# Weights in contiguous tiles, the first pair of the scan ahead of them, and low weight parts by TensorE

## The chip, the cores and the metric

The kernel runs on one core of one Trainium2 chip. What counts is the device time of the whole launch in microseconds; the median of several runs stands for a kernel. Inside the core five engines run their own in-order streams: TensorE (PE, with its weight loads PEld), VectorE (DVE), ScalarE (ACT), GpSimd (POOL) and SyncE (SP), which here issues all DMAs. They meet only at semaphores.

## The reference

The work is a gated linear attention (a complex-valued scan over time) followed by two MLPs. The MLP weights come as float64, which the kernel handles as pairs of 32-bit words.

```python
scale = min(mag, 0.999) / (mag + 1e-06)          # mag = |a_re + i a_im|
for t in range(768):                             # B=4, H=8, D=48
    new_re = ar * S_re - ai * S_im
    new_im = ar * S_im + ai * S_re
    S_re, S_im = new_re + k_t v_t^T, new_im
    y[:, :, t] = q_t @ S_re
x = y.transpose(0, 2, 1, 3).reshape(3072, 384)
x = square(relu(x @ w_in)) @ w_out               # w_in 384x2048
xn = x / rms(x) * rms_g
out = (silu(xn @ w_gate) * (xn @ w_val)) @ w_out2  # w_gate 384x1536
```

## The kernel before, in words

Time is cut into chunks of 128 steps, which makes 24 units (4 batches of 6 chunks); two units make a pair. For each pair `load_a`, `load_qk` and `load_v` bring the inputs, and a chain on VectorE and ScalarE works on the decay factors: `norm` (L131 to L155), seven times `step` (L165 to L170), `tot` (a TensorE product, L178), `blocks` (L199 to L206), `back` (L217), `apply` (L242 to L244) and `inv` (L255 to L258). Then each unit runs `kq` (the products KP and QP, L264), four turnings on TensorE (`dtr`, L286, copied out by ScalarE at L288), `score` (L298, copied at L300 and masked by GpSimd at L301), `do_y` (L314, copied as xt at L321), `fix` (six small transfers that regroup rows, L605), `state` (L332 to L346), and `split_x`, which cuts xt into a high part (ScalarE, L541) and a low part (VectorE, L542), called xs.

Two units make a group of 256 tokens for the first MLP: for each of the 16 blocks f of 128 hidden columns nine products of `mlp_h` (L620) and six of `mlp_x` (L637), with ScalarE and VectorE forming the high and low parts gs in between. All matrix products use such pairs (high x high, high x low, low x high) in the fp32r type. The second MLP has groups of three units and starts when the scan is done.

A weight tile of 128x384 has to be converted before use: a transfer lands the 64-bit words in `ws`, and `convert_f32` cuts them to 32 bits with one ScalarE step (L359), one GpSimd step (L360) and two VectorE steps (L363, L364) in one of two buffers `cr`; then ScalarE casts the high part (L541) and VectorE subtracts it to get the low part (L542). The first MLP has 32 such tiles, 16 of `w_in` and 16 of `w_out`. A `w_in` tile takes four transfers, since its rows are regrouped (`PIECES`, L560); a `w_out` tile takes one (L568). The second MLP has 36 tiles.

The order on each engine is not written by hand. Every step is entered with a time and a priority (`at(t, fn, ..., p=)`), the list is sorted by t, and a scheduler places the instructions by the priorities and by its own idea of what is free. `PSH`, `USH` and `WSH` shift the priorities of pair steps, unit steps and first-MLP conversions; the smaller number goes first.

Of the kernel before, what the change touches and what calls it, by code (L numbers as in the profile page):

```python
# [8 lines left out]
F32 = mybir.dt.float32  # L9
# [21 lines left out]
PSH, USH, WSH = -12, -4, -30  # L31
LOADA, LOADQ = -5, 7.5
YMAX2 = 3e4
GROUPS = [[2 * i, 2 * i + 1] for i in range(12)]
# [10 lines left out]
class Attention:  # L45
# [8 lines left out]
    def __init__(self, ctx, tc, q, k, v, a_re, a_im, ident, sb, ps, dram):  # L54
# [6 lines left out]
        self.V = [c.tile([128, H, 64], F32, name=f"V{i}") for i in range(2)]  # L61
# [10 lines left out]
    def init(self, mn):  # L72
# [13 lines left out]
        for t in self.V:  # L86
            nc.vector.memset(t[:, :, D:64], 0.0)
# [217 lines left out]
    def yy(self, u, xt):  # L305
# [5 lines left out]
        for p in range(4):  # L311
            for z in range(2):
                h = 2 * p + z
                nc.tensor.matmul(P[64 * z:64 * z + 64, p], lhsT=V[:, h, :], rhs=ST[:, h, :], start=True, stop=(c == 0))  # L314
# [8 lines left out]
    def state(self, u):  # L323
# [6 lines left out]
        for h in range(H):  # L330
            for lo, hi in ((0, 64), (64, 112)):
                nc.tensor.matmul(P[lo:hi, h], lhsT=kt[:, h, lo:hi], rhs=V[:, h, 0:D], start=True, stop=True)  # L332
# [48 lines left out]
def general_path(tc, q, k, v, a_re, a_im, w_in, w_out, w_gate, w_val, w_out2, ident, gcol, out):  # L381
# [3 lines left out]
    with ExitStack() as ctx:  # L385
        dram = ctx.enter_context(tc.tile_pool(name="g_dram", bufs=1, space=DRAM))
        xd = dram.tile([NT, DM], F32, name="g_xd")
        with ExitStack() as c1:
# [9 lines left out]
            with tc.For_i(0, S_LEN // T, 1) as it:  # L398
# [7 lines left out]
                for z in range(DQ):  # L406
                    nc.sync.dma_start(
                        vt[32 * z:32 * z + 32], v[:, :, bass.ds(it * T, T), :].rearrange("b h t d -> (b h) t d")
                    )
                re, im = tl["re"], tl["im"]  # L410
                flat = [t.rearrange("p t d -> p (t d)") for t in (re, im)]
                m, n, w = [sb.tile([128, T * DI], F32, name=f"g_m{i}") for i in range(3)]
# [34 lines left out]
        with ExitStack() as c2:  # L447
# [3 lines left out]
            def cols(w, f):  # L451
                st = sb.tile([128, KT, 256], I32, tag="gst", name="g_st", bufs=2)
                nc.sync.dma_start(st, w[:, 256 * f:256 * (f + 1)].rearrange("(k p) f -> p k f", p=128))
                return convert_f32(nc, sb, st.rearrange("p k n -> p (k n)")).rearrange("p (k n) -> p k n", k=KT)

            def rows(w, f):
                st = sb.tile([128, 2 * DM], I32, tag="gst", name="g_st", bufs=2)
                nc.sync.dma_start(st, w[128 * f:128 * (f + 1)])
                return convert_f32(nc, sb, st)
# [20 lines left out]
            with tc.For_i(0, NT // 128, 1) as it:  # L480
                x = sb.tile([128, DM], F32, tag="gx", name="g_x")
                nc.sync.dma_start(x, xd[bass.ds(it * 128, 128), :])
                xt = turned(x, None)
                acc = ps.tile([128, DM], F32, tag="gacc", name="g_acc")
                for f in range(F1):
                    hp = mm3(cols(w_in, f), xt, "gh")
# [3 lines left out]
                    nc.tensor.matmul(acc, lhsT=g, rhs=rows(w_out, f), start=(f == 0), stop=(f == F1 - 1))  # L490
# [8 lines left out]
                for f in range(F2):  # L499
                    gp = mm3(cols(w_gate, f), xt, "gh")  # L500
                    vp = mm3(cols(w_val, f), xt, "gv")
# [3 lines left out]
                    nc.tensor.matmul(acc, lhsT=g, rhs=rows(w_out2, f), start=(f == 0), stop=(f == F2 - 1))  # L505
# [6 lines left out]
def kernel_body(ctx: ExitStack, tc, q, k, v, a_re, a_im, w_in, w_out, w_gate, w_val, w_out2, rms_g, out):  # L512
    nc = tc.nc
    events = []
    w_in, w_out, w_gate, w_val, w_out2 = [t.bitcast(I32) for t in (w_in, w_out, w_gate, w_val, w_out2)]
# [6 lines left out]
    ident = keep.tile([128, 128], F32, name="ident")  # L522
    gcol = keep.tile([128, KT], F32, name="gcol")
# [28 lines left out]
    def load_cols(src, f, pieces, pool=wp):  # L552
        w = stage(pool)
        st = w[2].rearrange("p (k n) -> p k n", k=KT)
        if pieces is None:
            nc.sync.dma_start(st, src[:, 256 * f:256 * (f + 1)].rearrange("(k p) f -> p k f", p=128))
        else:
            width = src.shape[1]
            for r0, cnt, base, step in pieces:
                nc.sync.dma_start(  # L560
                    st[r0:r0 + cnt],
                    bass.AP(src.tensor, base * width + 256 * f, [[width, cnt], [step * width, KT], [1, 256]]),
                )
        return w

    def load_rows(src, f, pool=wp):
        w = stage(pool)
        nc.sync.dma_start(w[2], src[f * 128:(f + 1) * 128])  # L568
        return w

    def convert(w):
# [3 lines left out]
        split(w[:, 0], w[:, 1], r, nc.vector)  # L575
# [3 lines left out]
    PIECES = ((0, 48, 0, 96), (48, 16, 288, 16), (64, 48, 48, 96), (112, 16, 336, 16))  # L579
# [4 lines left out]
    def load_w1(f):  # L584
        win[f] = load_cols(w_in, f, PIECES)
        wout[f] = load_rows(w_out, f)

    def convert1(f, rows):
        w = wout if rows else win
        w[f] = convert(w[f])  # L590
# [268 lines left out]
```

## Time and profile before

| what | value |
|---|---|
| median of the runs | 1184.83 us (lowest 1183.83) |
| profiled execution, its own time | 1183.78 us |
| profiled execution, span from first to last instruction | 1182.1 us |
| TensorE matmul busy | 1060.9 us (90%) |
| VectorE busy | 720.7 us (61%) |
| ScalarE busy | 653.6 us (55%) |
| mean granted TensorE clock | 0.989 of full |

The shares are means over stages that differ: the page's slices show TensorE idle at the left end and nearly full from the fifth slice on, and VectorE full in the first third. What happens at the left end is read from windows of time and from the timeline.

### The profile page before, as it was taken

Reading aid. Unit: us, or ns where it says so; the run is one execution under the profiler, and the core shown is the slowest. Engines: PE = TensorE matmul, PEld = TensorE weight load, DVE = VectorE, ACT = ScalarE, POOL = GpSimd, SP = SyncE. Lnnn points to the kernel's source line nnn. Section 1 sums busy time; section 2 is a strip of 40 time slices with the busy share of each in tenths; the row PEclk is TensorE's granted clock in tenths of the full one; section 3 lists DMA queues with packets and bytes.
Section 4 is the critical chain, followed back from the end, with each engine's and each line's share of the span. In section 5 each row is a group of like instructions: output and inputs, shape, how many; then the busy total and the mean of one; then the engine's idle time right before and its main releaser. Section 6 shows DMA issues by size and latency. Waiting matters only on the chain.

```text
span 1182.1 us, 20622 instructions
## 1 busy us (share of the span) xinstructions
PE 1060.9 (90%) x7778; PEld 1030.7 (87%) x7778; DVE 720.7 (61%) x1564; ACT 653.6 (55%) x1421; POOL 210.9 (18%) x246
## 2 busy tenths in 40 slices
PE   0015898999999999999999999999999999999997
PEld 0014788999999999999999999999999999999997
DVE  6999797988978779687842379932232323222222
ACT  4347576786786767877577676733232424222221
POOL 2335342323222333222200023200000000000000
PEclk9998799999999999999999999999999999999999
DMA  9933322423423234231100493000000000000000
GB/s 230 250 88 85 101 60 89 113 70 99 126 58 110 65 84 108 76 110 38 44 24 16 142 313 117 21 21 21 21 21 21 21 21 21 21 3 18 16 6 23
DMA packets 98748, 85.45 MB, mean 72 GB/s; under 512 B 53328, under 2 KB 92496, under 8 KB 98640
## 3 DMA queue, kind: packets, MB, share of 16 engines
q1 hardware_dynamic: 98640, 84.05, 25.3%
q8 instruction: 63, 1.03, 0.4%
q14 instruction: 45, 0.37, 0.1%
HBM read 64.23 MB, written 18.61 MB: 70 GB/s over the span
## 4 chain that ended last, share of the span: by engine, by line
PE 58%; DVE 17%; ACT 9%; issue 6%; DMA 6%; SPq 3%; POOL 2%; DVEq 0%; ACTq 0%; POOLq 0%
PE o L789 12%; PE v L771 11%; PE g L771 11%; PE h L620 8%; PE x L637 8%; DVE XY L165 2%; PE sps L298 2%; DMA ws<-in_moe_w_in 2%; SPq L605 2%; PE dps L286 1%; DMA ws<-in_moe_w_out 1%; DVE cr L363 1%; PE yps L314 1%; DVE cr L364 1%; ACT dq L288 1%
## 5 line engine op out<-in xcount | busy, mean ns | idle before, releaser
L620 PE MATMUL h<-xs,w 128*128 128x256 f32 x1728 | 331.3, 287 | 10.3 <-ACT xs L541 6.1
L637 PE MATMUL x<-w,gs 128*128 128x384 f32 x1152 | 315.1, 348 | 9.1 <-DVE gs L627 8.6
L620 PEld LDWEIGHTS h<-xs,w 128*128 128x128 f32 x1728 | 269.5, 192 | 14.0 <-ACT xs L541 6.5
L637 PEld LDWEIGHTS x<-w,gs 128*128 128x128 f32 x1152 | 202.1, 190 | 15.0 <-DVE gs L627 11.4
L777 DVE TENSOR_TENSOR uu<-t,v 128x384 f32<-128x384 f32 x96 | 52.9, 552 | 206.9 <-PE v L771 204.0
L771 PE MATMUL g<-ys,w 128*128 128x384 f32 x864 | 171.7, 339 | 0.0
L789 PE MATMUL o<-w,us 128*128 128x384 f32 x864 | 170.8, 340 | 0.1
L771 PE MATMUL v<-ys,w 128*128 128x384 f32 x864 | 170.5, 340 | 0.3 <-DVE uu L777 0.3
L771 PEld LDWEIGHTS v<-ys,w 128*128 128x128 f32 x864 | 153.1, 188 | 0.9 <-DVE uu L777 0.6
L771 PEld LDWEIGHTS g<-ys,w 128*128 128x128 f32 x864 | 153.5, 188 | 0.3 <-ACT t L775 0.3
L789 PEld LDWEIGHTS o<-w,us 128*128 128x128 f32 x864 | 151.8, 188 | 1.0 <-ACT us L541 0.4
L775 ACT ACTIVATE t<-g 128x384 f32<-128x384 f32 x96 | 47.0, 490 | 146.0 <-PE g L771 146.0
L627 DVE TENSOR_TENSOR gs<-h,gs 128x256 fp32r<-128x256 f32 x192 | 79.4, 417 | 77.4 <-ACT h L626 74.9
L541 ACT CAST us<-uu 128x384 fp32r<-128x384 f32 x96 | 49.2, 513 | 114.1 <-DVE uu L777 114.1
L623 ACT ACTIVATE r<-h 128x256 f32<-128x256 f32 x192 | 73.6, 386 | 61.1 <-PE h L620 60.3
L360 POOL TENSOR_SCALAR cr<-ws 128x384 f32<-128x384 f32 x68 | 56.4, 834 | 155.8 <-DVE w L542 94.4
L625 ACT ACTIVATE gs<-r 128x256 fp32r<-128x256 f32 x192 | 81.2, 423 | 3.8
L301 POOL TENSOR_SCALAR_AFFINE_SELECT st<-st 128x512 f32<-128x512 f32 x48 | 38.7, 811 | 232.4 <-ACT st L300 231.7
L542 DVE TENSOR_TENSOR us<-uu,us 128x384 fp32r<-128x384 f32 x96 | 54.3, 566 | 38.3 <-ACT us L541 38.3
L626 ACT ACTIVATE h<-r 128x256 f32<-128x256 f32 x192 | 73.1, 381 | 0.0
L178 PE MATMUL tot<-ident,A 128*48 128x128 f32 x96 | 9.1, 305 | 57.9 <-DVE A L169 57.9
L165 DVE TENSOR_TENSOR XY<-A 128x384 f32<-128x384 f32 x84 | 59.0, 702 | 1.0
(117 smaller groups left out, 1485.8 us busy)
## 6 DMA issues: line engine op xcount, KB each, us to landing
ws<-in_moe_w_out SPq DMA_DIRECT2D x28, 384.0 KB, 5.3
kb<-KP SPq DMA_DIRECT2D x20, 448.0 KB, 4.1
kt<-kb SPq DMA_DIRECT2D x20, 448.0 KB, 4.1
raw<-in_a_re SPq DMA_DIRECT2D x24, 192.0 KB, 3.1
raw<-in_a_im SPq DMA_DIRECT2D x24, 192.0 KB, 3.3
ws<-in_moe_w_in SPq DMA_DIRECT2D x32, 144.0 KB, 5.1
kin<-in_k SPq DMA_DIRECT2D x24, 192.0 KB, 4.3
qin<-in_q SPq DMA_DIRECT2D x24, 192.0 KB, 3.1
```

The source lines that it names most:

```text
L165: nc.vector.tensor_tensor(out=T, in0=v.unsqueeze(1).to_broadcast([128, 2, 2, 2 * D]), in1=w.unsqueeze(2).to_broadcast([128, 2, 2, 2 * D]), ...
L360: nc.gpsimd.tensor_scalar(out=s.bitcast(F32), in0=hi.bitcast(F32), scalar1=0.0, scalar2=1.0, op0=ALU.mult, op1=ALU.mult)
L542: el.tensor_tensor(out=lo, in0=src, in1=hi.bitcast(F32), op=ALU.subtract)
L620: nc.tensor.matmul(hp, lhsT=w[:, a, kk, :], rhs=xs[:, bb, kk, :], start=(i == 0), stop=(i == 8))
L623: nc.scalar.activation(out=r, in_=hp, func=AF.Relu)
L625: nc.scalar.activation(out=gs[:, 0], in_=r, func=AF.Square)
L626: nc.scalar.activation(out=hp, in_=r, func=AF.Square)
L627: nc.vector.tensor_tensor(out=gs[:, 1], in0=hp, in1=gs[:, 0].bitcast(F32), op=ALU.subtract)
L637: nc.tensor.matmul(x_ps[g][i], lhsT=gs[:, a, i * CH:(i + 1) * CH], rhs=w[:, bb, :], start=(f == 0 and n == 0), stop=(f == F1 - 1 and n == 2),)
L771: nc.tensor.matmul(P, lhsT=w[:, a, kk, :], rhs=ys[:, bb, kk, :], start=(i == 0), stop=(i == 8))
L777: nc.vector.tensor_tensor(out=uu, in0=t, in1=ps[1], op=ALU.mult)
L789: nc.tensor.matmul(o_ps[g][i], lhsT=us[:, a, i * CH:(i + 1) * CH], rhs=w[:, bb, :], start=(f == 0 and n == 0), stop=(f == F2 - 1 and n == 2),)
```

## The change

The host now lays all five weight matrices out as one array of 128x768-word tiles in the order of use, so that each tile, of either kind, is one transfer with 3 KB rows (`load`). V is laid out on the host too, one row of 384 numbers for a time step, and its tile has no gaps of zeros any more. The loads of pairs 0 and 1 and the steps of the first pair and its units get priorities of their own (`LOAD0`, `PAIR0`, `UNIT0`), ahead of the conversions; the conversions of the first MLP move from `WSH` -30 to -40. Last, the low part of a first-MLP weight tile is formed on TensorE: identity times the 32-bit weights in fp32, plus minus-identity times the high part in fp32r, summed in PSUM (in the buffers of `h`), and ScalarE copies the result out. The second MLP's tiles keep the VectorE subtraction. The path for unusual inputs, which does not run here, is adapted and left out below.

```diff
-PSH, USH, WSH = -12, -4, -30
+PSH, USH, WSH = -12, -4, -40
+PAIR0, UNIT0 = -60, -50
+LOAD0 = ((-64, -63, -62.5), (-36.35, -35.5, -35.2))
...
-        self.V = [c.tile([128, H, 64], F32, name=f"V{i}") for i in range(2)]
+        self.V = [c.tile([128, H * D + 16], F32, name=f"V{i}") for i in range(2)]
...
-            self.V[u % 2][:, :, 0:D],
-            self.v[b, :, c * CH:(c + 1) * CH, :].rearrange("h t e -> t h e"),
+            self.V[u % 2][:, 0:H * D], self.v[b, c * CH:(c + 1) * CH].rearrange("t h e -> t (h e)")
...
+    minus = keep.tile([128, 128], F32R, name="minus")
...
+    def load(n, pool=wp):
+        t = stage(pool)
+        nc.sync.dma_start(t[2], w[n])
+        return t
+
+    def convert(w, on_pe):
+
         pool, n, st = w
         r = convert_f32(nc, CV[0], st, "cr", CRB)
         w = pool.tile([128, 2, DM], F32R, tag=f"w{n}", name="w", bufs=1)
-        split(w[:, 0], w[:, 1], r, nc.vector)
+        if not on_pe:
+            split(w[:, 0], w[:, 1], r, nc.vector)
+            return w
+        nc.scalar.copy(out=w[:, 0], in_=r)
+        P = psh.tile([128, DM], F32, tag="h", name="lo")
+        nc.tensor.matmul(P, lhsT=ident, rhs=r, start=True, stop=False)
+        nc.tensor.matmul(P, lhsT=minus, rhs=w[:, 0], start=False, stop=True)
+        nc.scalar.copy(out=w[:, 1], in_=P)
         return w
...
     def load_w1(f):
-        win[f] = load_cols(w_in, f, PIECES)
-        wout[f] = load_rows(w_out, f)
+        win[f] = load(T_IN + f)
+        wout[f] = load(T_OUT + f)
...
-        at(F1 * (g - 3) + LOADA, att.load_a, g)
-        at(F1 * (g - 2) + LOADQ, att.load_qk, g)
+        t = F1 * (g - 3) + LOADA
+        at(t, att.load_a, g, p=LOAD0[g][0] if g < 2 else t)
+        t = F1 * (g - 2) + LOADQ
+        at(t, att.load_qk, g, p=LOAD0[g][1] if g < 2 else t)
         for fr, *op in PAIR:
             t = F1 * (g - 2 + fr)
-            at(t, getattr(att, op[0]), g, *op[1:], p=t + PSH)
+            at(t, getattr(att, op[0]), g, *op[1:], p=t + PSH if g else PAIR0 + 10 * fr)
...
+                p = t0 + F1 * fr + USH if g else UNIT0 + 3 * i + 4 * fr
```

In what order the engines get the work stands in the built programs. On SyncE's queue, at the very start, the kernel before has this (the first number in a shape is partitions):

```order
L108 DMA raw<-in_a_re 128x1x384 x2
L108 DMA raw<-in_a_im 128x1x384 x2
L560 DMA ws<-in_moe_w_in 48x3x256
L560 DMA ws<-in_moe_w_in 16x3x256
L560 DMA ws<-in_moe_w_in 48x3x256
L560 DMA ws<-in_moe_w_in 16x3x256
L568 DMA ws<-in_moe_w_out 128x768
```

and the changed kernel this:

```order
L112 DMA raw<-in_a_re 128x1x384 x2
L112 DMA raw<-in_a_im 128x1x384 x2
L120 DMA kin<-in_k 128x1x384 x2
L120 DMA qin<-in_q 128x1x384 x2
L126 DMA V_89<-in_v 128x384
L126 DMA V_90<-in_v 128x384
L563 DMA ws<-in_w 128x768 x16
L112 DMA raw<-in_a_re 128x1x384 x2
L112 DMA raw<-in_a_im 128x1x384 x2
L563 DMA ws<-in_w 128x768 x16
```

The inputs k, q and v of the first pair, which stood behind all weights, now stand ahead of the first one.

On VectorE, in the first pair's `norm` and first `step`, the kernel before has this:

```order
L149 TENSOR_TENSOR m<-m,A_86 128x768
L542 TENSOR_TENSOR w<-cr,w 128x384 x2
L150 SCALAR_TENSOR_TENSOR A_86<-m,A_86 128x768
L363 SCALAR_TENSOR_TENSOR cr<-ws,cr 128x384 x2
L364 SCALAR_TENSOR_TENSOR cr<-cr 128x384
L152 SCALAR_TENSOR_TENSOR m<-A_86 128x768
L364 SCALAR_TENSOR_TENSOR cr<-cr 128x384
L542 TENSOR_TENSOR w<-cr,w 128x384
L155 TENSOR_TENSOR A_86<-raw,m 128x768 x2
```

and the changed kernel this:

```order
L152 TENSOR_TENSOR m<-m,A_87 128x768
L153 SCALAR_TENSOR_TENSOR A_87<-m,A_87 128x768
L366 SCALAR_TENSOR_TENSOR cr<-ws,cr 128x384
L367 SCALAR_TENSOR_TENSOR cr<-cr 128x384
L366 SCALAR_TENSOR_TENSOR cr<-ws,cr 128x384
L155 SCALAR_TENSOR_TENSOR m<-A_87 128x768
L367 SCALAR_TENSOR_TENSOR cr<-cr 128x384
L158 TENSOR_TENSOR A_87<-raw,m 128x768 x2
```

The subtractions `w<-cr,w` are gone, and the pair's chain comes earlier among the conversions.

On TensorE, around the first product of the first MLP, the changed kernel has this (in the kernel before 27 products `h` stand there without a break, and no `lo`):

```order
L317 MATMUL yps<-st,V_90 64x128 x4
L622 MATMUL h<-xs,w 128x256
L576 MATMUL lo<-cr,ident 128x384
L577 MATMUL lo<-w,minus 128x384
L576 MATMUL lo<-cr,ident 128x384
L577 MATMUL lo<-w,minus 128x384
L622 MATMUL h<-xs,w 128x256 x17
```

Of the 32 new pairs of products 28 stand ahead of this place, two in it, and two a little behind it, among the first group's products.

## Rows read from the trace of the kernel before

**Rows 1.** The page: busy time by engine, and the span in 40 slices.

```profile
PE 1060.9 (90%) x7778; PEld 1030.7 (87%) x7778; DVE 720.7 (61%) x1564; ACT 653.6 (55%) x1421; POOL 210.9 (18%) x246
...
PE   0015898999999999999999999999999999999997
...
DVE  6999797988978779687842379932232323222222
```

**Rows 2.** Windows: stretch and length, busy by engine, granted clock, DMA share, GB/s.

```profile
0.00:125.40 125.40, 25.54 (x189) 20.05 (x189) 107.38 (x237) 64.01 (x119) 50.99 (x54) 0.94 0.63 154
...
125.50:181.25 55.75, 49.24 (x409) 47.52 (x410) 51.77 (x111) 39.60 (x87) 18.38 (x19) 0.95 0.30 85
181.25:650.00 468.75, 462.75 (x4106) 444.65 (x4105) 356.66 (x789) 345.42 (x766) 116.66 (x136) 1.00 0.28 78
```

**Rows 3.** Timeline of PE and DVE: first products of the first two groups.

```profile
119.68 2.29 PE L620 MATMUL h<-xs,w 128*128 128x256 f32 x9 [6.11 <-ACT xs L541]
125.51 4.21 PE L620 MATMUL h<-xs,w 128*128 128x256 f32 x18 [3.55 <-DVE xs L542]
...
180.63 0.62 PE L637 MATMUL x<-w,gs 128*128 128x384 f32 x2 [3.68 <-DVE gs L627]
...
123.63 0.56 DVE L363 SCALAR_TENSOR_TENSOR cr<-ws,cr 128x384 int32<-128x384 int32 x1 [3.12 <-POOL cr L360]
124.11 1.35 DVE L542 TENSOR_TENSOR xs<-xt,xs 128x384 fp32r<-128x384 f32 x1
```

**Rows 4.** Windows of the start: the DMA share and rate stand last.

```profile
20.00:60.00 40.00, 1.26 (x8) 0.86 (x8) 36.58 (x93) 15.79 (x30) 12.61 (x12) 1.00 1.05 250
60.00:80.00 20.00, 1.78 (x10) 1.06 (x10) 19.43 (x43) 10.27 (x22) 6.20 (x6) 1.00 0.36 90
```

**Rows 5.** VectorE: the subtractions (ns min/median/max; group's mean), a 128x768 step.

```profile
L542 DVE TENSOR_TENSOR w<-cr,w x68: 539/549/1350, 13.8 to 766.0; 128x384 fp32r<-128x384 f32 x68
...
L542 DVE TENSOR_TENSOR w<-cr,w 128x384 fp32r<-128x384 f32 x68 | 41.3, 613 | 3.9 <-ACT w L541 3.9
...
L155 DVE TENSOR_TENSOR A<-raw,m 128x768 f32<-128x768 f32 x24 | 23.4, 1016 | 0.2
...
13.76 1.02 DVE L542 TENSOR_TENSOR w<-cr,w 128x384 fp32r<-128x384 f32 x2
```

**Rows 6.** ScalarE: first conversion step in the timeline, and two groups.

```profile
9.30 0.55 ACT L359 ACTIVATE cr<-ws 128x384 f32<-128x384 f32 x1 [0.61 <-DMA ws<-in_moe_w_in]
...
L541 ACT CAST w<-cr 128x384 fp32r<-128x384 f32 x68 | 34.6, 512 | 39.6 <-DVE cr L364 39.1
...
L648 ACT COPY x<-x 128x384 f32<-128x384 f32 x12 | 5.7, 477 | 5.4 <-PE x L637 5.4
```

**Rows 7.** Timeline of PE: an fp32 and an fp32r form, early and late.

```profile
91.44 3.78 PE L298 MATMUL sps<-dq,dk 112*128 112x128 f32 x16 [0.93 <-ACT dq L288]
...
129.52 1.48 PE L637 MATMUL x<-w,gs 128*128 128x384 f32 x4
...
139.93 1.95 PE L298 MATMUL sps<-dq,dk 112*128 112x128 f32 x16
...
155.44 0.87 PE L637 MATMUL x<-w,gs 128*128 128x384 f32 x4
```

**Rows 8.** Windows of 10 us: ScalarE's busy time is fourth, the granted clock third from the end.

```profile
100.00:110.00 10.00, 4.64 (x31) 3.52 (x32) 10.00 (x13) 9.51 (x17) 6.76 (x8) 0.85 0.18 40
...
120.00:130.00 10.00, 6.45 (x29) 6.16 (x29) 6.88 (x9) 2.88 (x9) 7.05 (x7) 0.50 0.09 24
130.00:140.00 10.00, 9.26 (x66) 8.91 (x65) 9.53 (x26) 9.18 (x19) 0.79 (x1) 0.95 0.80 244
180.00:190.00 10.00, 9.37 (x60) 9.32 (x61) 7.38 (x20) 6.47 (x14) 0.00 (x0) 0.83 0.60 187
```

More of the change, by code (lines that the diff above doesn't have):

```diff
@@ L313, in yy @@
                 h = 2 * p + z
-                nc.tensor.matmul(P[64 * z:64 * z + 64, p], lhsT=V[:, h, :], rhs=ST[:, h, :], start=True, stop=(c == 0))
+                nc.tensor.matmul(P[64 * z:64 * z + 64, p], lhsT=V[:, h * D:h * D + 64], rhs=ST[:, h, :], start=True, stop=(c == 0))
             if c > 0:
@@ L331, in state @@
             for lo, hi in ((0, 64), (64, 112)):
-                nc.tensor.matmul(P[lo:hi, h], lhsT=kt[:, h, lo:hi], rhs=V[:, h, 0:D], start=True, stop=True)
+                nc.tensor.matmul(P[lo:hi, h], lhsT=kt[:, h, lo:hi], rhs=V[:, h * D:(h + 1) * D], start=True, stop=True)
         t = self.tmp("sWY").rearrange("p (z h e) -> p z h e", z=2, h=H)
@@ L378, in rsqrt, with general_path @@
     return y
[L381 removed]
+def general_path(tc, q, k, v, a_re, a_im, w, ident, gcol, out):
     nc = tc.nc
@@ L481, in general_path @@
                 x = sb.tile([128, DM], F32, tag="gx", name="g_x")
-                nc.sync.dma_start(x, xd[bass.ds(it * 128, 128), :])
+                for kk in range(KT):
+                    for r0, cnt, base, step in PIECES:
+                        nc.sync.dma_start(
+                            x[:, kk * 128 + r0:kk * 128 + r0 + cnt],
+                            xd[bass.ds(it * 128, 128), base + step * kk:base + step * kk + cnt],
+                        )
                 xt = turned(x, None)
@@ L489, in general_path @@
                     nc.vector.tensor_tensor(out=g, in0=g, in1=g, op=ALU.mult)
-                    nc.tensor.matmul(acc, lhsT=g, rhs=rows(w_out, f), start=(f == 0), stop=(f == F1 - 1))
+                    nc.tensor.matmul(acc, lhsT=g, rhs=words(T_OUT + f), start=(f == 0), stop=(f == F1 - 1))
                 x1 = sb.tile([128, DM], F32, tag="gx1", name="g_x1")
@@ L504, in general_path @@
                     nc.vector.tensor_tensor(out=g, in0=g, in1=vp, op=ALU.mult)
-                    nc.tensor.matmul(acc, lhsT=g, rhs=rows(w_out2, f), start=(f == 0), stop=(f == F2 - 1))
+                    nc.tensor.matmul(acc, lhsT=g, rhs=words(T_OUT2 + f), start=(f == 0), stop=(f == F2 - 1))
                 o = sb.tile([128, DM], F32, tag="go", name="g_o")
@@ L511, in kernel_body @@
 @with_exitstack
-def kernel_body(ctx: ExitStack, tc, q, k, v, a_re, a_im, w_in, w_out, w_gate, w_val, w_out2, rms_g, out):
+def kernel_body(ctx: ExitStack, tc, q, k, v, a_re, a_im, w, rms_g, out):
     nc = tc.nc
+    w = w.bitcast(I32)
     events = []
-    w_in, w_out, w_gate, w_val, w_out2 = [t.bitcast(I32) for t in (w_in, w_out, w_gate, w_val, w_out2)]
     def at(t, fn, *a, p=None):
@@ L822, in kernel_body @@
     att.init(mn)
+    nc.scalar.mul(minus, ident, -1.0)
     nc.sync.dma_start(gcol, rms_g.rearrange("(k p) -> p k", p=128))
@@ L831, in kernel_body, with weight_tiles, cols @@
     with tc.If(good < 1):
-        general_path(tc, q, k, v, a_re, a_im, w_in, w_out, w_gate, w_val, w_out2, ident, gcol, out)
-_INS = [
-    "q", "k", "v", "a_re", "a_im", "moe_w_in", "moe_w_out",
-    "moe2_w_gate", "moe2_w_val", "moe2_w_out", "moe2_rms_g",
-]
+        general_path(tc, q, k, v, a_re, a_im, w, ident, gcol, out)
+def weight_tiles(inputs):
+    import numpy as np
+    rows = np.concatenate([
+        np.concatenate([np.arange(base + step * k, base + step * k + n) for _, n, base, step in PIECES]) for k in range(KT)
+    ])
+    def cols(w):
+        return w.reshape(KT, 128, -1, 128).transpose(2, 1, 0, 3).reshape(-1, 128, DM)
+    a = [np.asarray(inputs["moe_" + n]) for n in ("w_in", "w_out")]
+    a += [np.asarray(inputs["moe2_" + n]) for n in ("w_gate", "w_val", "w_out")]
+    tiles = [cols(a[0][rows]), a[1].reshape(-1, 128, DM), cols(a[2]), cols(a[3]), a[4].reshape(-1, 128, DM)]
+    return np.ascontiguousarray(np.concatenate(tiles)).view(np.int64)
 def kernel(**inputs):
```

82 lines of the change are left out of this document (33 added, 49 removed).

## The prediction

> **What bounds the kernel now.** Read the page's shares first, then its slices: TensorE's 90% hides two stages [rows 1]. It is nearly idle in the first three of 40 slices and full from the fifth on, while VectorE is full at the left end. The windows put numbers on this [rows 2]. From 181 to 650 us TensorE is busy for 462.75 of 468.75 us: nothing but TensorE work counts there, and the change adds none to that stretch. Up to 125.4 us TensorE is busy for 25.5 us and VectorE for 107.4 us. The timeline shows how the start ends [rows 3]: the first products `h` begin at 119.68, stop for the low part of xs and run on from 125.51, since VectorE, a step behind, does that part only at 124.11. So the start is paid in VectorE time: whatever leaves VectorE there moves the dense stretch of TensorE forward. The group after that (125.5 to 181.25) is mixed: TensorE 49.2 of 55.75 us, VectorE 51.8 [rows 2], ended by a wait of 3.68 us for VectorE's gs [rows 3].
>
> **One transfer for each tile.** I cost it at nothing. The DMA engines are saturated from 20 to 60 us (share 1.05, 250 GB/s) and drop to 0.36 in the next 20 us [rows 4]: the weights are all in by about 62 us, while the first dense product comes at 125.5, so landing is no bound later on. What hides it is VectorE's own pace. The V tile without gaps feeds the same products; the second MLP's tiles are converted as before, beside a full TensorE.
>
> **The first pair's loads ahead of the weights.** Six transfers of 192 KB (k, q, v), 1.18 MB, now stand ahead of the first weight. At 250 GB/s [rows 4] that is 4.7 us, so the first conversion, at 9.30 us before [rows 6], comes at about 14. VectorE has only the pair's `norm` until then and idles where it had four conversion steps of about half a microsecond (0.56 for one [rows 3]): I take 2 us, between 0 and 4.7.
>
> **The low parts by TensorE.** In the order of the kernel before, 28 of the 32 subtractions stand ahead of the second xs. One takes 0.549 us (median), 0.48 where two follow each other, 0.613 as the mean with its stretched cases [rows 5]: 28 x 0.55 = 15.4 us, between 13.4 and 17.2. The changed order has, ahead of the same point, two more `apply`-sized steps of `norm` (L155, 1.0 us each [rows 5]), a `step` product and a conversion step (of the same 128x384 size, 0.5 each) and one step of `inv` less (1.0): 2.0 us back. VectorE's busy time to that point goes from 107.4 to 107.4 - 15.4 + 2.0 = 94.0 us.
>
> What comes in place of it: an identity product in fp32, a minus-identity product in fp32r and a ScalarE copy, for each tile. For the fp32 price the nearest row is `sps`, 16 passes of 128 columns: 3.78 us early, 1.95 us late, 0.236 and 0.122 a pass [rows 7]. The built form makes two passes of each fp32 product (16 for 8 products), and 384 columns are three times 128, so six such units: 1.42 us at the early speed and 0.73 at the late one. The fp32r product is an `x` product: 1.48 / 4 = 0.37 early, 0.87 / 4 = 0.22 late. TensorE has 100 idle us ahead of 125.4 and takes 28 x 1.8 = 50 us there at the low speed without being full. Only what others wait for counts:
>
> The two buffers `cr`. Before, a buffer was held by cast and subtraction, 0.512 + 0.549 = 1.06 us [rows 5, 6]; now until the identity product has read it, 1.42 us, or 0.73 at the high speed. That is +0.36 or -0.33 for each tile; with two buffers half of it can show, 28 / 2 x 0.36 = +5 to -4.6 us. VectorE's work between two conversions is 94 / 30 = 3.1 us, longer than that hold, so I take +1.
>
> ScalarE's copies. A copy of this shape out of PSUM takes 0.477 us [rows 6], 28 of them 13.4 us, and each stands in ScalarE's in-order queue until TensorE is through, with the copies of `dps` and the steps of `norm` and `inv` behind it, for which VectorE and TensorE wait. ScalarE is busy for 64 of 125.4 us [rows 2], so most of it lies beside other work; but from 100 to 110 us, where the units' turnings are copied, it is busy for 9.5 of 10 [rows 8]. About six copies fall in the corresponding stretch of the new order: 6 x 0.477 = 3 us, between 0 and 13.4.
>
> VectorE's idle time to 125.4 us is 18.0 us [rows 2]. With 2 + 1 + 3 it becomes 24.0, and xs is ready at 94.0 + 24.0 = 118.0 us: a gain of **7.4 us**.
>
> **The first group.** TensorE needs its 49.2 us and about 1.8 for the two late pairs of `lo` (0.73 + 0.22 each); VectorE is relieved of four subtractions (2.2 us), and the changed order has three `step`s and four gs fewer ahead of the next xs, so its 51.8 us fall below TensorE's 51. I leave 1.5 us of the 6.5 us of idle time: 52.5 instead of 55.75, a gain of **3.2 us**, between -1.8 (idle stays) and 4.7. What is late next is TensorE itself.
>
> **The granted clock.** From 180 to 190 us it is 0.83 on average [rows 8]: 3.4 us at 1.2 instead of 2.4 GHz, right behind the 3.68 us of waiting. If the wait goes, so does the dip: **1.7 us**, between 0 and 1.7.
>
> **The sum.** 7.4 + 3.2 + 1.7 = 12.3 us off the profiled execution's 1183.78, which is its span of 1182.1 and 1.7 around it, and 1.05 below the median: 1171.5 there, **1172 us** as a median. The ends of all terms together: VectorE +-1.9, start 0 to 4.7, buffers -4.6 to +5, ScalarE 0 to 13.4, group -1.8 to 4.7, dip 0 to 1.7, which is 1184.8 - (7.4 + 1.9 + 2 + 5.6 + 3 + 4.7 + 1.7) = 1158.5 to 1184.8 - (7.4 - 1.9 - 2.7 - 4 - 10.4 - 1.8) = 1198.2.
>
> **Rivals.** (1) *All of VectorE's gain arrives.* No added wait shows (the buffers are free in time, ScalarE has room): 13.4 us at xs, 3.2 and 1.7 as above: 1166.5. With the clock up when `h` begins it is more. Before, `h` began at a granted 0.50, which lasted until about 131 us [rows 8]; its 5.4 us from 125.5 on were half lost, 2.7 us. TensorE had been idle for most of the 6 us ahead [rows 3]; now `lo` pairs fill such gaps. 1166.5 - 2.7 = 1163.8, and with 5.6 us more from shorter holds at the high speed 1158. For it: ScalarE's 64 us and TensorE's 25; against it: the full ScalarE from 100 to 110. By the Trainium skill ("TensorE: Matmul & The Clock Gate", section "What's actually happening") the throttled clock is the default and activity releases it; the trace agrees, with 0.50 granted behind the idle stretch and 0.95 in the next ten, and by that rule alone the forecast would be 1169.
>
> (2) *The chain of latencies sets the start, not VectorE's sum.* Turnings, scores, masks and `fix` run TensorE to ScalarE to GpSimd to SP and back. If the new products and copies between them cost as much as the splits gave, xs comes at 123 to 127 us and only the group's 0 to 3 us remain: 1180 to 1188. For it: the 3.12 us wait for GpSimd just ahead of xs [rows 3], which no term removes.
>
> (3) *The conversions become the pace, and it is slower than before.* Each tile now goes VectorE, TensorE, ScalarE, with ScalarE standing still for TensorE's slow clock. The place is ScalarE's queue from 10 to 118 us; the price the upper bounds of start, buffers and copies, 4.7 + 5 + 13.4 = 23.1 us against the 13.4 net of VectorE, and the group's 1.8: 1184.8 + 9.7 + 1.8 = 1196. It decides from about 0.42 us of new waiting for each of 32 tiles on. Against it: ScalarE's half-idle start.
>
> (4) *The order does not do what it says*: excluded for the first pair, whose loads and steps do stand ahead in the built queues; for the transfers it is what I assume, no gain.
>
> **How the numbers follow.** The forecast (1164.5 to 1180) gets 0.53, rival 1 below that 0.17, rival 2 0.20, rival 3 0.10. The range 1159 to 1186 leaves out the last two or three us of rival 1, the tail of rival 2 and rival 3, about 0.15. A change of 2%, which is about what a measurement of this kernel can tell from none, is 23.7 us, to 1161.1 or 1208.5: below it lies the better half of rival 1 and some of what I cannot see, 0.15; above it, 0.04; between them 0.81.
>
> **What would show it.** In the trace after: first `h` products without a stop from about 118 us on; VectorE busy for about 94 us up to there; no L542 rows on `w` in the first 120 us; identity products of about 0.7 us a pass at first; a first group of 52 to 53 us without the 3.68 us wait. The forecast is wrong if VectorE idles for more than 30 us up to xs, with ScalarE or GpSimd's L363 as the releaser, if ScalarE's copies out of `lo` lead its waits, or if TensorE loses time behind 181 us, where I assume nothing changes.

## The result, and the profile after

The changed kernel takes **1170.72 us** (median; 1169.68 to 1171.03), where 1172 had been forecast. Beside runs of the kernel before on the same chip (median 1184.84 us) the ratio is 0.9882, 95% interval 0.9865 to 0.9899: 14 us less. That is inside the 2% that the prediction named as no change, but the interval keeps well clear of 1, so here a gain of 1.2% can be told from none. The profiled execution has a span of 1169.3 us, 12.8 less than before.

The page of the changed kernel (busy time by engine, slices of the span, DMA packets), to be held against [rows 1]:

```profile
PE 1097.5 (94%) x7874; PEld 1047.1 (90%) x7874; DVE 708.5 (61%) x1532; ACT 665.2 (57%) x1454; POOL 199.5 (17%) x246
...
PE   3566999999999999999999999999999999999997
...
DVE  6999898897877978779741489823232323222222
...
PEclk9777999999999999999999999999999999999999
...
DMA packets 66237, 85.46 MB, mean 73 GB/s; under 512 B 27984, under 2 KB 54864, under 8 KB 66128
```

TensorE works from the first slice on, where it was idle before, and VectorE's row at the left end is as full as it was. That is the first thing to see: the new TensorE work is in the stretch that had room for it, and VectorE is still what fills that stretch.

Windows of the changed kernel, to be held against [rows 2] (up to the low part of the second xs, from there to the point where as many products `h` and `x` together are recorded as before at 181.25 us, 250 and 248, and on to 650):

```profile
0.00:117.30 117.30, 64.42 (x273) 37.67 (x273) 102.55 (x212) 77.01 (x153) 43.14 (x56) 0.80 0.52 171
117.40:174.30 56.90, 52.67 (x439) 50.16 (x440) 49.80 (x116) 42.98 (x92) 16.47 (x17) 0.97 0.34 100
174.30:650.00 475.70, 469.20 (x4188) 451.53 (x4187) 352.81 (x784) 346.90 (x778) 116.31 (x138) 1.00 0.25 74
```

The timeline of TensorE and VectorE in the changed kernel, against [rows 3]:

```profile
112.79 0.58 PE L622 MATMUL h<-xs,w 128*128 128x256 f32 x1 [6.11 <-ACT xs L550]
117.36 2.04 PE L622 MATMUL h<-xs,w 128*128 128x256 f32 x15 [0.94 <-DVE xs L551]
...
124.23 0.65 PE L289 MATMUL dps<-ident,KP 128*112 128x128 f32 x4 [1.47 <-ACT dk L291]
148.54 2.68 PE L301 MATMUL sps<-dq,dk 112*128 112x128 f32 x16 [2.23 <-ACT dq L291]
...
116.41 0.89 DVE L551 TENSOR_TENSOR xs<-xt,xs 128x384 fp32r<-128x384 f32 x1
```

The first product still waits 6.11 us, as before, `lo` products fill the gap behind it, and the dense stretch begins at 117.36 instead of 125.51. The wait of 3.68 us for gs is gone; one of 2.23 us for a turned block stands at 148.5.

What VectorE waits for ahead of 168.45 us in the changed kernel (engine, line waited for, us in total, times, longest):

```profile
DVE m L135 <- ACT A L134: 4.7, 1, 4.7
DVE cr L366 <- POOL cr L363: 3.6, 5, 1.2
DVE gs L629 <- ACT h L628: 2.8, 3, 1.2
DVE pX L207 <- ACT TP L185: 2.2, 2, 1.6
```

and what leads the same list of the kernel before, ahead of 181.25 us:

```profile
DVE cr L363 <- POOL cr L360: 7.4, 11, 3.1
```

In the changed kernel no copy out of `lo` and no TensorE product leads this list. GpSimd does wait for the identity product, 28.6 us in all, but seldom long enough for VectorE to feel it:

```profile
POOL cr L363 <- PE lo L576: 28.6, 13, 5.7
```

**One account for all kernels.** The last 1000.85 us of a kernel (what follows 181.25 us in the kernel before) hold 986.10 us of TensorE work before and 986.17 after, and between 983.8 and 989.0 in every kernel below. So, to within some 3 us of TensorE work, all that differs lies ahead of that point, a stretch called the start from here on. It is 181.25 us before and 168.45 after, and it can be written as VectorE's busy plus its idle time. That sum is bookkeeping; what tells something is which of the two moves. The windows of the start in four kernels (before, changed, split_on_vector and no_sign; VectorE's busy time is the third of the five):

```profile
0.00:181.25 181.25, 74.78 (x598) 67.56 (x599) 159.25 (x347) 103.61 (x206) 69.46 (x72) 0.94 0.53 133
0.00:168.45 168.45, 111.28 (x668) 82.03 (x669) 146.78 (x310) 114.34 (x235) 59.71 (x72) 0.85 0.45 144
0.00:180.75 180.75, 79.30 (x607) 72.76 (x608) 160.48 (x340) 103.73 (x208) 70.28 (x72) 0.92 0.42 135
0.00:155.75 155.75, 106.80 (x649) 78.43 (x650) 134.93 (x307) 112.58 (x232) 36.48 (x36) 0.86 0.47 153
```

And all kernels:

| kernel | ratio to before (95%) | start, us | VectorE busy | idle | TensorE busy |
|---|---|---|---|---|---|
| before | 1 | 181.25 | 159.25 | 22.0 | 74.8 |
| changed kernel | 0.9882 (0.9865 to 0.9899) | 168.45 | 146.78 | 21.7 | 111.3 |
| split_on_vector | 1.0 (0.9988 to 1.0011) | 180.75 | 160.48 | 20.3 | 79.3 |
| tiles_only | 0.999 (0.9977 to 1.0003) | 179.75 | 154.67 | 25.1 | 77.5 |
| order_of_before | 0.9937 (0.992 to 0.9953) | 173.65 | 142.47 | 31.2 | 118.3 |
| low_by_tensor_only | 0.9908 (0.9892 to 0.9925) | 172.35 | 143.29 | 29.1 | 119.2 |
| no_sign | 0.9745 (0.9728 to 0.9763) | 155.75 | 134.93 | 20.8 | 106.8 |
| sign_on_scalar | 0.9857 (0.9841 to 0.9874) | 166.35 | 144.45 | 21.9 | 112.7 |
| three_cr | 0.9918 (0.9901 to 0.9935) | 171.55 | 148.24 | 23.3 | 110.3 |
| lo_copy_on_vector | 0.9936 (0.9919 to 0.9952) | 175.45 | 154.72 | 20.7 | 117.4 |
| lo_twice | 0.9951 (0.9931 to 0.997) | 174.65 | 145.80 | 28.9 | 124.4 |
| late_loads | 0.9899 (0.9882 to 0.9915) | 170.65 | 145.03 | 25.6 | 118.5 |
| half_sign | 0.9877 (0.9859 to 0.9894) | 163.15 | 137.66 | 25.5 | 110.5 |
| warm_tensor | 0.9993 (0.9983 to 1.0003) | 180.05 | 156.17 | 23.9 | 106.6 |

The ratio comes from several runs, the other columns from the one profiled execution, which in no_sign was 2.0 us above the median of its runs and in half_sign 2.2 us below. Times below are the ratio by 1184.84 us. A caution for all of them: the scheduler places instructions anew with each edit, so a kernel differs from its parent in more than the edit.

### The profile page after: what moved, and what is told of

It reads as the page before. It is cut to its first block, busy times and chain, and to the rows that moved or that the text cites. A ratio compares the mean times of both kernels' runs of the same rounds, so it can differ in the third digit from the quotient of the medians.

```text
span 1169.3 us, 20736 instructions
## 1 busy us (share of the span) xinstructions
PE 1097.5 (94%) x7874; PEld 1047.1 (90%) x7874; DVE 708.5 (61%) x1532; ACT 665.2 (57%) x1454; POOL 199.5 (17%) x246
## 3 DMA queue, kind: packets, MB, share of 16 engines
q8 instruction: 64, 1.05, 0.4%
## 4 chain that ended last, share of the span: by engine, by line
PE 63%; DVE 18%; ACT 8%; issue 4%; SPq 2%; DMA 1%; POOL 0%; DVEq 0%; ACTq 0%; POOLq 0%
PE o L794 12%; PE g L776 12%; PE v L776 12%; PE x L639 10%; PE h L622 10%; DVE XY L168 3%; PE sps L301 2%; SPq L607 2%; PE dps L289 2%; DVE cr L366 1%; DVE KP L267 1%; ACT dk L291 1%; PE yps L317 1%; DVE cr L367 1%; ACT dq L291 1%
## 5 line engine op out<-in xcount | busy, mean ns | idle before, releaser
L622 PE MATMUL h<-xs,w 128*128 128x256 f32 x1728 | 326.0, 284 | 7.1 <-ACT xs L550 6.1
L622 PEld LDWEIGHTS h<-xs,w 128*128 128x128 f32 x1728 | 265.8, 189 | 10.2 <-ACT xs L550 6.4
L576 PE MATMUL lo<-cr,ident 128*128 128x384 f32 x64 | 39.6, 711 | 38.3 <-DVE cr L367 38.2
L363 POOL TENSOR_SCALAR cr<-ws 128x384 f32<-128x384 f32 x68 | 48.4, 714 | 145.2 <-DVE w L551 52.5
```

Of the source, the lines that this page charges most:

```text
L622: nc.tensor.matmul(hp, lhsT=w[:, a, kk, :], rhs=xs[:, bb, kk, :], start=(i == 0), stop=(i == 8))
```

## The experiments

### Which part of the change makes the gain

**split_on_vector**: the changed kernel with VectorE's subtraction back.

```diff
-        w[f] = convert(w[f], True)
+        w[f] = convert(w[f], False)
```

> The changed kernel with the low parts of the first MLP's weights back on VectorE; tiles, early loads and order stay. Theory (the start is paid in VectorE time, and the 28 subtractions are the gain): ahead of the second xs VectorE gets 24 subtractions back and, in the built order, leaves 9 conversion steps for later, so xs comes at 117.3 + 24 x 0.55 - 9 x 0.5 = about 126 us, and the first group, with VectorE at 49.8 of 56.9 us, gets 8 subtractions and 9 steps more and grows: 1180 to 1188 us. Rival (the early loads and the new order make the gain, the low parts are worth nothing): xs stays below 120 us and the time is 1168 to 1174 us.

1184.8 us: the whole gain is gone, as the theory said. But not by its steps: the dense products begin at 115.98 us, earlier than in the changed kernel, while the subtractions are paid for behind them. Timeline of TensorE:

```profile
115.98 3.79 PE L622 MATMUL h<-xs,w 128*128 128x256 f32 x18 [1.82 <-DVE xs L551]
128.44 1.01 PE L639 MATMUL x<-w,gs 128*128 128x384 f32 x2 [5.35 <-DVE gs L629]
...
177.23 4.96 PE L622 MATMUL h<-xs,w 128*128 128x256 f32 x27 [3.19 <-ACT xs L550]
```

A start that looks 1.4 us better at its first dense product costs 12 us more. The moment of xs, on which the prediction built its largest term, is not what the start costs. VectorE's work up to the steady stretch tells more: it is 13.7 us longer here than in the changed kernel. (The granted clock behind xs differs too; see the part on the clock below.)

**tiles_only**: as above, and the old priorities.

```diff
-PSH, USH, WSH = -12, -4, -40
+PSH, USH, WSH = -12, -4, -30
...
-        at(t, att.load_a, g, p=LOAD0[g][0] if g < 2 else t)
+        at(t, att.load_a, g)
...
-            at(t, getattr(att, op[0]), g, *op[1:], p=t + PSH if g else PAIR0 + 10 * fr)
+            at(t, getattr(att, op[0]), g, *op[1:], p=t + PSH)
...
-                p = t0 + F1 * fr + USH if g else UNIT0 + 3 * i + 4 * fr
+                p = t0 + F1 * fr + USH
```

> Only the tiles (one transfer each, and V's layout): order and priorities of the kernel before, low parts on VectorE. Theory (landing is no bound): 1182 to 1187 us, though the weights are in some 15 us earlier, as in the changed kernel. Rival (part of the gain is that weights land sooner): 1172 to 1179 us.

1183.7 us, as the theory said, though the transfers are much faster (below). Its first dense product comes at 109.97 us, the earliest of the first four kernels here, and it gains nothing from that either.

**order_of_before**: tiles and low parts by TensorE, priorities as in tiles_only.

> The changed kernel with the priorities of the kernel before: tiles and low parts by TensorE stay, the first pair's loads stand behind the weights again. Theory (the gain is the VectorE time of the subtractions): 1169 to 1176 us, the first dense product at 115 to 122 us. Rival (the order makes the gain): 1179 to 1186 us, the first dense product behind 123 us.

1177.4 us, between the two, 1.4 us above the theory's range; the dense products begin at 115.75 us, as the theory had it. VectorE works less than in the changed kernel (142.5 us), but idles for 31.2 instead of 21.7: it waits 7.7 us for `h` from ScalarE and 7.2 for GpSimd's step on `cr`, 2.8 and 3.6 in the changed kernel.

**low_by_tensor_only**: the kernel before with the low parts by TensorE and nothing else.

```diff
...
-        split(w[:, 0], w[:, 1], r, nc.vector)
+        if not on_pe:
+            split(w[:, 0], w[:, 1], r, nc.vector)
+            return w
+        nc.scalar.copy(out=w[:, 0], in_=r)
+        P = psh.tile([128, DM], F32, tag="h", name="lo")
+        nc.tensor.matmul(P, lhsT=ident, rhs=r, start=True, stop=False)
+        nc.tensor.matmul(P, lhsT=minus, rhs=w[:, 0], start=False, stop=True)
+        nc.scalar.copy(out=w[:, 1], in_=P)
         return w
...
-        w[f] = convert(w[f])
+        w[f] = convert(w[f], True)
```

> The kernel before with the low parts by TensorE alone: four transfers for a w_in tile, old order. Theory (VectorE time): 1169 to 1177 us. Rival (low parts on TensorE only shift the wait to ScalarE and TensorE, and tiles or order make the gain): 1181 to 1188 us. If it is much above the kernel with tiles and low parts, late transfers hold the tiles on the longer way.

1173.9 us: this part alone brings 0.92% of the 1.18%. Its VectorE is relieved by 16.0 us in the start and idles 7.1 us more. Its dense products begin later than those of the kernel before (125.51), and it is faster all the same:

```profile
126.21 4.06 PE L628 MATMUL h<-xs,w 128*128 128x256 f32 x22
```

The tiles add nothing to it: with them, in the same order (order_of_before), the ratio is 0.9937 against 0.9908, with intervals that just meet.

**late_loads**: the changed kernel with k, q and v of the first pair behind the weights, the steps' priorities kept.

```diff
-        at(t, att.load_qk, g, p=LOAD0[g][1] if g < 2 else t)
+        at(t, att.load_qk, g)
```

(and the same for `load_a` and `load_v`)

> The changed kernel without the early loads: k, q and v of the first pair behind the weights again, the priorities of the first pair's steps stay. The first conversion comes at about 9.7 us as in the kernel before (13.1 in the changed one), so VectorE idles some 3 us less at the left end. If the early loads gain nothing by themselves: 1166 to 1171 us. If the gain of the order over the old one (1176.4 to 1170.7 us) rests on k, q and v being there: 1174 to 1178 us, with VectorE idle for 28 us or more up to the second group.

1172.9 us; its interval covers the changed kernel's 0.9882. No gain of the early loads can be told from none.

### Whether VectorE's time is what counts

**lo_copy_on_vector**: VectorE copies the low part out of PSUM.

```diff
-        nc.scalar.copy(out=w[:, 1], in_=P)
+        nc.vector.tensor_copy(w[:, 1], P)
```

> The changed kernel with the low part copied out of PSUM by VectorE in place of ScalarE: VectorE gets 32 steps of about 0.5 us back, ScalarE loses as many. Theory (VectorE's time is the gain): 1180 to 1187 us, no gain left. Rival (what counts is where the low part is formed, or ScalarE's copies hold the start up): 1165 to 1174 us.

1177.3 us: the direction of the theory, about half its size. The 32 copies take 17.5 us on VectorE (548 ns each), its busy time in the start rises by 7.9, and the start by 7.0. Of the other 9.6 us some 2.5 are the spacing of the copies, which follow the step before them by 0.47 us (as worked out below); the rest is mostly that five other steps fewer stand ahead of the point and that GpSimd stretches VectorE's steps less (see no_sign).

**no_sign**: GpSimd's step of the conversion left out.

```diff
-    nc.gpsimd.tensor_scalar(
-        out=s.bitcast(F32), in0=hi.bitcast(F32), scalar1=0.0, scalar2=1.0, op0=ALU.mult, op1=ALU.mult
-    )
-    nc.vector.scalar_tensor_tensor(out=s, in0=lo, scalar=29, in1=s, op0=ALU.logical_shift_right, op1=ALU.bitwise_or)
+    zero = s if zero is None else zero
+    nc.vector.scalar_tensor_tensor(out=s, in0=lo, scalar=29, in1=zero, op0=ALU.logical_shift_right, op1=ALU.bitwise_or)
...
+    nc.vector.memset(zero, 0)
```

> The changed kernel without GpSimd's step of every conversion, which makes the sign: the sign of the weights is left out, and VectorE reads a tile of zeros in its place, so its own steps stay the same. In the changed kernel's start every VectorE step that is stretched (33 up to 117 us, 14 us in all, 0.33 us the usual one) lies beside a GpSimd step. Theory (GpSimd's steps stretch VectorE's, and VectorE's time sets the start): 32 x 0.33 = 10.6 us of VectorE time less up to the second group, 1158 to 1164 us, and the means of L366 and L367 at 0.55. Rival (the chain of latencies sets the start, or the stretching has another cause): 1168 to 1173 us.

1154.6 us, below the theory's range and far from the rival's. VectorE's busy time in the start falls by 11.85 us, for 10.6 expected. How the stretching looks in the changed kernel's timeline of VectorE and GpSimd:

```profile
28.05 0.55 DVE L168 TENSOR_TENSOR XY<-A 128x384 f32<-128x384 f32 x1
...
28.10 0.88 POOL L363 TENSOR_SCALAR cr<-ws 128x384 f32<-128x384 f32 x1 [0.72 <-ACT w L574]
...
30.51 0.55 POOL L363 TENSOR_SCALAR cr<-ws 128x384 f32<-128x384 f32 x1 [1.53 <-PE lo L576]
30.59 0.88 DVE L367 SCALAR_TENSOR_TENSOR cr<-cr 128x384 int32<-128x384 int32 x1
```

At 28.05 VectorE is first and GpSimd's step takes 0.88 us instead of 0.55; at 30.51 GpSimd is first and VectorE's step takes 0.88 instead of 0.55. In both the later one pays. By the Trainium skill ("SBUF — State Buffer", section "SBUF: two separate sides") a VectorE step with two SBUF inputs and a GpSimd step that reads SBUF contend for one pair of ports, which the first holds for its whole instruction; these rows agree: the later step ends 0.38 and 0.41 us after the earlier one, 0.33 us late. The two VectorE lines of the conversion, in the start, first in the changed kernel (columns: busy us, mean ns, idle before):

```profile
L367 DVE SCALAR_TENSOR_TENSOR cr<-cr 128x384 int32<-128x384 int32 x32 | 20.4, 639 | 1.2 <-ACT cr L362 0.6
L366 DVE SCALAR_TENSOR_TENSOR cr<-ws,cr 128x384 int32<-128x384 int32 x32 | 18.9, 590 | 3.6 <-POOL cr L363 3.6
```

and then without GpSimd's step:

```profile
L364 DVE SCALAR_TENSOR_TENSOR cr<-ws,zero 128x384 int32<-128x384 int32 x32 | 17.8, 566 | 3.1 <-DMA ws<-in_w 1.6 <-PE lo L575 0.9 <-ACT w L573 0.4
L365 DVE SCALAR_TENSOR_TENSOR cr<-cr 128x384 int32<-128x384 int32 x32 | 17.5, 551 | 0.6 <-ACT cr L362 0.5
```

These two lines give 4.0 us of the 11.85; most of the rest is in the steps of the pair's chain that stood beside a GpSimd step. Measured against the lower quartile of the same form, VectorE's steps in the start are stretched by 18.4 us in the changed kernel (43 of them by over 0.15 us) and by 8.5 us here (14), and each of those lies beside a GpSimd step.

**sign_on_scalar**: the same step on ScalarE. ScalarE's product with zero does not keep the sign, so this kernel too computes without it.

```diff
-    nc.gpsimd.tensor_scalar(
-        out=s.bitcast(F32), in0=hi.bitcast(F32), scalar1=0.0, scalar2=1.0, op0=ALU.mult, op1=ALU.mult
-    )
+    nc.scalar.activation(out=s.bitcast(F32), in_=hi.bitcast(F32), func=AF.Copy, scale=0.0)
```

> The changed kernel with the conversion's GpSimd step on ScalarE: 32 steps of about 0.5 us more there, VectorE no longer stretched by them. If VectorE's time alone sets the start, as without the sign: 1158 to 1164 us. If ScalarE, busy for 114 of the first 168 us, can't take 16 us more beside its copies: 1168 to 1178 us.

1167.9 us, at the lower edge of the second case and 13 us worse than without the step at all. ScalarE is busy for 129.3 of 166.35 us, 17.6 of them in the new step, and VectorE waits 5.1 us for that step. VectorE's steps are stretched less, as expected (12.9 us, 20 of them by over 0.15), but 11 more of them stand ahead of the point (321 against 310), so its busy time falls by 2.3 us only. Of the 16 us that leaving the step out brings, 3 are left.

**half_sign**: that for the 16 `w_out` tiles alone, with a bias of minus zero (an attempt at a better kernel).

```diff
-        w[f] = convert(w[f], True)
+        w[f] = convert(w[f], True, negz if rows else None)
...
+        nc.scalar.activation(out=s.bitcast(F32), in_=hi.bitcast(F32), func=AF.Identity, bias=neg, scale=0.0)
```

> The changed kernel with GpSimd's step on ScalarE for the 16 w_out tiles alone (times zero, plus minus zero, which keeps the sign). Theory: VectorE is stretched by 16 x 0.33 = 5.3 us less, and ScalarE, busy for 114 of the first 168 us, takes 8 us more: 1163 to 1168 us, better than the changed kernel and than all steps on ScalarE. Rival (every ScalarE step added costs what it relieves): 1169 to 1172 us.

1170.3 us, the rival's range: no better than the changed kernel. The step takes 636 ns with its bias against 549 in sign_on_scalar, and, to judge by its output, the sign of these 16 tiles is not kept here either, so no better version came of it. (Its profiled execution took 1165.81 us, its runs 1168.05 in the median, so its row in the table flatters it.)

### What else could bound the start

**lo_twice**: both products of each low part issued twice.

```diff
         nc.tensor.matmul(P, lhsT=minus, rhs=w[:, 0], start=False, stop=True)
+        nc.tensor.matmul(P, lhsT=ident, rhs=r, start=True, stop=False)
+        nc.tensor.matmul(P, lhsT=minus, rhs=w[:, 0], start=False, stop=True)
```

> The changed kernel with both products of every low part issued twice into the same PSUM buffer (the second pair overwrites the first): TensorE gets 32 x 1.0 us (clock up) to 1.8 us (clock down) more, and every cr buffer is held and every ScalarE copy delayed by as much. Theory (VectorE's time sets the start, TensorE and the holds lie beside it): 1169 to 1175 us. Rival (the way of a tile through TensorE and ScalarE is close to the pace, the third rival of the prediction): 28 x half of 1.0 to 1.8 us shows, 1184 us or more.

1179.0 us, between the two. VectorE's busy time falls by 1 us and its idle time rises by 7.2. Waits of VectorE and GpSimd in its start:

```profile
POOL cr L363 <- PE lo L578: 42.9, 15, 5.7
...
DVE cr L366 <- POOL cr L363: 8.0, 10, 2.7
DVE pX L207 <- ACT TP L185: 7.5, 3, 4.9
```

GpSimd waits 42.9 us for the products instead of 28.6, and VectorE 4.4 us more for GpSimd and 5.3 more for a ScalarE copy. So the way through TensorE is not free without limit: once does not show in VectorE's idle time (21.7 us, 22.0 before), twice costs 8 us. Nor is once wholly off the path: the chain of work followed back from the end of the changed kernel's start passes through identity products for 4.9% of it.

**three_cr**: a third buffer for the half of `cr` that the identity product reads.

```diff
-    rs = pool.tile([128, 2 * DM], I32, tag=tag, name="cr", bufs=bufs)
-    r, s = rs[:, 0:DM], rs[:, DM:2 * DM]
+    r = pool.tile([128, DM], I32, tag=tag, name="cr", bufs=bufs + 1)
+    s = pool.tile([128, DM], I32, tag=tag + "s", name="crs", bufs=bufs)
```

> The changed kernel with three buffers in place of two for the half of cr that the identity product reads. GpSimd's step waits 28.6 us in all for that product to release a buffer. Theory (VectorE finds other work meanwhile, its 21.7 us of idle time up to 168 us are mostly the first 14 us and ScalarE's chain): 1167 to 1172 us. Rival (the hold of the buffers is the pace): 1158 to 1165 us.

1175.1 us, slower than both had it. GpSimd no longer waits for the product (it waits 32.6 us for VectorE's L367 instead), and no time comes of it, which speaks against the rival. Why it loses 4 us is not settled: VectorE works 1.5 us more and idles 1.6 more, in another order.

**warm_tensor**: split_on_vector with products that keep TensorE at work and relieve nobody.

```diff
+            if warm:
+                P = psh.tile([128, DM], F32, tag="h", name="lo")
+                for i in range(4):
+                    nc.tensor.matmul(P, lhsT=minus, rhs=w[:, 0], start=(i == 0), stop=(i == 3))
...
+        w[f] = convert(w[f], False, True)
```

> The kernel with the low parts back on VectorE (1183.5 us), and four products of minus-identity with each high part whose result nobody reads: TensorE is kept at work in the start, VectorE is not relieved. If the granted clock at the first dense products is part of the changed kernel's gain: 1178 to 1181 us. If VectorE's time sets the start whatever the clock: 1182 to 1186 us, with the granted clock above 0.9 in the first group.

1184.0 us, but its condition failed: the granted clock was not up in the first group (third from the end).

```profile
110.00:120.00 10.00, 3.23 (x10) 2.65 (x10) 9.87 (x17) 3.23 (x6) 1.02 (x2) 0.67 0.28 83
120.00:130.00 10.00, 2.73 (x14) 2.10 (x13) 7.75 (x13) 3.53 (x7) 8.99 (x7) 0.67 0.00 1
130.00:140.00 10.00, 8.75 (x49) 7.92 (x50) 9.56 (x24) 5.39 (x11) 3.64 (x2) 0.78 0.43 131
```

So it says nothing of what the clock is worth. It does show that 27 us more of TensorE work ahead of the steady stretch bring nothing by themselves.

## Why the prediction held, and where its steps did not

**The bound** was named rightly. Giving VectorE steps back takes the gain away in whole (split_on_vector) or in half (lo_copy_on_vector), relieving it further brings more (no_sign), and the idle time stays between 20.3 and 21.9 us in five kernels, split_on_vector, lo_copy_on_vector, the changed kernel, sign_on_scalar and no_sign, while the busy time goes from 160.5 down to 134.9; TensorE's lies anywhere between 79 and 117. It is not the only thing that counts: idle time is 22.0 us in the kernel before and 23.3 to 31.2 in the other eight, and there it takes back part of what VectorE is relieved of.

**One transfer for each tile, at nothing**: right, and for the reason given. The weights land sooner than the prediction thought possible; windows of the changed kernel, against [rows 4]:

```profile
20.00:50.00 30.00, 20.58 (x48) 9.56 (x48) 28.07 (x72) 22.69 (x51) 11.20 (x14) 0.84 0.91 318
50.00:60.00 10.00, 4.27 (x8) 1.96 (x7) 9.88 (x16) 3.51 (x7) 1.75 (x2) 0.67 0.26 79
```

They are in before 50 us instead of 62, and tiles_only gains nothing from it. The 250 GB/s of [rows 4] was no ceiling, though: from 20 to 50 us 318 GB/s moved, at a lower share.

**The early loads, 2 us**: the first conversion comes at 13.12 us (14 forecast). VectorE is idle for 9.2 us to there, for 7.5 to 9.30 before: 1.7 us. late_loads shows that nothing that can be measured hangs on it.

**The low parts, 7.4 us at xs**: xs came at 117.3 us (118.0 forecast), by two errors that cancelled. VectorE's busy time to that point was 102.55 us, not 94.0. One part of it: the price of 0.55 us for a subtraction is its duration, but back-to-back steps start 0.47 us apart (28.63, 29.10, 29.57 in no_sign's timeline), so 28 of them free 13.2 us, not 15.4. Another: the stretching, which the prediction priced only as part of the subtractions (0.613 as the mean with stretched cases), so as to leave with them. It did not leave: measured against the lower quartile of the same form, steps up to xs were stretched by about 9.5 us before (21 of them by over 0.15 us) and 14 to 15 after (33 to 37, by how forms are told apart), every one beside a GpSimd step, while GpSimd's own step of the conversion went from 1039 to 778 ns in the mean up to there. So GpSimd more often came first and VectorE paid. That does not follow from the low parts alone: with them on TensorE in the old order it is 11.0 us up to xs in low_by_tensor_only and 10.2 in order_of_before. What in the changed order makes it, no run isolates. Some 1 to 2 us of the 8.5 stay unplaced. Against that the idle time was 14.75 us, not 24.0: the 3 us for ScalarE's copies and the 1 for the buffers did not show up, and the wait of 3.12 us for GpSimd just ahead of xs [rows 3], which no term removed, is gone.

The prices on TensorE were too low: a pair of identity passes takes 1.65 us at the low clock and 0.91 at the high one (1.42 and 0.73 forecast), the minus product 0.75 in the mean (0.37 and 0.22). It did not show in VectorE's idle time, as the step had it; lo_twice shows that the margin is less than a second helping.

**The first group, 52.5 us**: wrong. By the count of `h` and `x` products it takes 56.9 us, 1.1 more than before: the 3.68 us wait went, but its TensorE work grew from 49.24 to 52.67 us and 4.2 us of idle time stand in it. It holds the two late pairs of `lo`, and 80 products L289 are done at its end where 64 were before. From this point to the end it is 995.0 us, 5.85 less than before, where the prediction had nothing change: the 16 products more are missing there (1.8 us), and so is the dip of the clock behind 180 us (1.7 us); the rest is not placed. So the term that failed is this split; 8.1 - 1.15 + 5.85 makes the 12.8 us, as 7.4 + 3.2 + 1.7 made 12.3. That the sum came out within half a microsecond is luck: the bound was right, its split was not.

**The clock**: the dip behind 180 us is gone, but a new one stands at 149.7, right behind the wait of 2.23 us:

```profile
149.70:153.20 3.50, 3.50 (x17) 3.50 (x17) 3.50 (x6) 3.28 (x5) 1.83 (x2) 0.51 0.00 0
...
120.00:130.00 10.00, 8.54 (x57) 7.65 (x58) 8.67 (x24) 6.87 (x13) 0.00 (x0) 1.00 0.62 179
```

The 1.7 us were moved, not gained. Rival 1's condition came true (granted 1.00 from 117.4 us on to this dip, 0.50 from 120 to 131 us before), yet its 1164 us did not: of its 13.4 us at xs 8.1 came, and of its 3.2 in the first group nothing.

The clock behind xs is a rival for part of the gain. From the second xs to 650 us TensorE is busy at half the clock for 8.9 us in the kernel before and 3.4 in the changed one, for 14.2 in split_on_vector, 17.4 in tiles_only, 9.4 in lo_copy_on_vector and 8.5 in no_sign; half of that is the most that the lower level can have cost directly. So up to 2.7 of the 12.8 us, and up to 5.4 of the 12.3 between split_on_vector and the changed kernel, may be the clock's. It does not order the kernels: tiles_only loses 4.3 us more in this way than the kernel before and its start is 1.5 us shorter, no_sign loses 2.6 more than the changed kernel and its start is 12.7 shorter. Which share it has is not settled.

One reading of the rows misleads: ahead of the first stretch of TensorE work a granted 1.00 is not what the products felt. In the changed kernel the window from 20 to 30 us has 1.00 as a whole, but the pairs of identity passes at 20.99 and 24.96 us took 1.65 us and those at 27.04 and 29.45 took 0.91.

**The rivals.** The second (a chain of latencies) has no_sign against it, which removes VectorE time and no latency that VectorE had been waiting long for: 3.6 us in all. It keeps a share in the old order, where VectorE idles for 29 to 31 us once TensorE makes the low parts; there the priorities, those of the first pair's steps and of the conversions, bring back most of a further 0.5% (0.9937 in order_of_before, 0.9899 in late_loads), and without the low parts they bring nothing (1.0 against 0.999). The third did not come: it needed 0.42 us of new waiting for each tile, and VectorE's idle time in the start did not grow. The fourth holds for the transfers.

## What to carry to other kernels

When one engine fills the start, price an edit by that engine's whole work up to the steady stretch, not by the moment at which the first product of the stretch begins: tiles_only had its first dense product 7 us ahead of the changed kernel's and ended 11 us behind it, and low_by_tensor_only had it 0.7 us behind that of the kernel before and ended 9 us ahead. Count a step at the distance between starts, not at its duration, and look at what stretches the engine's other steps: here the step of another engine, for which VectorE waited only 3.6 us in all, was worth more (16 us) than the whole change (14 us). Work moved to an idle engine is free only up to a point, so try it doubled.

## What was not expected of the hardware

- Sent as rows of 3 KB instead of rows of 1 KB (`w_in`) mixed with rows of 3 KB, the weights moved at 360 to 362 GB/s from 20 to 40 us in split_on_vector, at a DMA share of 1.04 to 1.05, where that share moved 250 before [rows 4] and 236 to 245 in low_by_tensor_only. Row size, number of transfers and partitions that one transfer reaches (48 or 16 against 128) changed together, so which of them does it is open.
- Of a VectorE step and a GpSimd step that overlap, the later one can take 0.88 us in place of 0.55, on either side. It is not so each time: in the changed kernel's start 111 VectorE steps overlap a GpSimd step, and 43 are stretched by over 0.15 us.
- ScalarE's product with zero did not keep the sign (sign_on_scalar); to judge by the output, a bias set to minus zero did not mend it (half_sign), and whether the bias reached the engine as such is open.
